# An adaLN block with segmented attention and a gated feed-forward: instruction order by list scheduling at build time, V stationary in column tiles, transposes moved off TensorE

## The chip, the cores and the metric

The kernel runs on one core of one Trainium2 chip. The metric is the device time in microseconds (us). The kernel before takes 308.86 us (median of 3 runs, 307.05 to 309.61). The profile is one further execution, with a span of 305.5 us. In the profile PE is TensorE's matmuls, PEld its weight loads, DVE is VectorE, ACT is ScalarE, POOL is GpSimd and SP is SyncE, which issues most of the DMAs.

## What is computed

The input x is 2048 rows of 448 numbers in bf16. A conditioning vector c gives six modulation vectors. The first half is attention in 16 heads of 28 numbers, in 4 segments of 512 rows. Within a segment it is causal softmax attention. Beside it stands a memory M that sums phi(k) times v over all earlier segments, and each head blends the two. The second half is a feed-forward with 1792 hidden columns.

```
sa, ca, ga, sb, cb, gb = (silu(c) @ w_mod).reshape(6, 448)

h = layernorm(x) * (1 + ca) + sa
q, k, v = h @ wq, h @ wk, h @ wv              # 16 heads of 28, 4 segments of 512 rows
phi(t) = t + 1 where t > 0, else exp(t)
for each segment s:
    p     = softmax(q_s k_s^T / sqrt(28) + causal mask)
    a_dot = p v_s
    a_mem = phi(q_s) M / (phi(q_s) z + 1e-6)  # M and z of the segments before s
    o_s   = g * a_mem + (1 - g) * a_dot       # g = sigmoid(beta), one number for each head
    M, z  = M + phi(k_s)^T v_s, z + sum phi(k_s)
x = x + ga * (o @ wo)

h = layernorm(x) * (1 + cb) + sb
x = x + gb * ((sigmoid(h @ w_gate) * (h @ w_up)) @ w_down)
```

(The reference blends with a_mem = 0 in the first segment, where M and z are zero.)

## The kernel before

The width of 448 is cut into 4 chunks of 112 partitions. Sixteen attention units, 4 segments of 4 head groups, are run through one after the other. Between their steps a queue of other work (`fill`) is served in order, by a quota of estimated TensorE nanoseconds. The parts that the change touches:

```python
# LayerNorm: statistics on VectorE, power -0.5 on GpSimd, normalised rows xn;
# turned on TensorE against an identity, then modulated on the way out of PSUM
def h_chunk(xns, hT, kc, vi, act_kc=(1, 3)):
    pt = m_bf16("lntr")
    for t in range(TPS):
        nc.tensor.transpose(pt[0:KP, t * P:(t + 1) * P], xns[t][:, kc * KP:(kc + 1) * KP], ident[:])      # L229
    if kc in act_kc:
        nc.scalar.activation(hT[:, kc, :], pt[0:KP, 0:L], AF.Identity, scale=..., bias=...)                 # L231
    else:
        nc.vector.tensor_scalar(hT[:, kc, :], pt[0:KP, 0:L], ..., op0=ALU.mult, op1=ALU.add)                # L234

# Q leaves PSUM through ScalarE, K through VectorE
if eng == "act": nc.scalar.copy(dst[:, hc, :], pq[:, 0:L])
else:            nc.vector.tensor_copy(dst[:, hc, :], pq[:, 0:L])                                           # L276

# memory: K turned on TensorE, then phi
ptk = m_bf16("ptk")
for hc in range(NHC):
    nc.tensor.transpose(ptk[:, hc * P:(hc + 1) * P], kT_of[s][:, hc, t * P:(t + 1) * P], ident[:])          # L294
nc.scalar.activation(ek[:], ptk[:, 0:512], AF.Exp)
nc.vector.tensor_scalar(ek[:], ek[:], 1.0, None, op0=ALU.min)                                               # L299
nc.vector.scalar_tensor_tensor(pk_of[s][:, t, :], ptk[:, 0:512], 0.0, ek[:], op0=ALU.max, op1=ALU.add)      # L300

# logits: four heads at once in row tiles; then exp, then the causal mask on GpSimd
nc.tensor.matmul(lg[:, hs, wid:wid + nq], lhsT=kT[r, hc, ...], rhs=qT[r, hc, kb * P:L], tile_position=(HP * hs, 0))
nc.scalar.activation(pT[:, :, w0:w0 + wid], lg[:, :, 0:wid], AF.Exp, scale=scale)                           # L341
nc.gpsimd.affine_select(out=blk, in_=blk, compare_op=ALU.is_ge, fill=0.0, ...)                              # L353

# P times V: P is stationary, V moves, 29 columns in each of 40 matmuls
for qb in range(TPS):
    for hs in range(4):
        for kb in range(qb + 1):
            nc.tensor.matmul(accv[:, qb, hs, 0:ME], lhsT=pT[:, hs, c0:c0 + P],
                             rhs=vt[:, kb, hc * 4 + hs, 0:ME], start=(kb == 0), stop=(kb == qb))            # L366
for qb in range(TPS):                                                                                       # memory read
    nc.tensor.matmul(memv[:, qb, :, 0:ME], lhsT=pq[:, qb * P:(qb + 1) * P], rhs=rm_of[s][:, hc, :, :], ...) # L373
# ... reciprocals, scales, two products (L379 to L399), their sum on GpSimd (L400)

# the output rows turned on TensorE, copied by VectorE
nc.tensor.transpose(op[0:KP, t * P:(t + 1) * P], ou[:, t, :, :]..., ident[:])                               # L408
nc.vector.tensor_copy(oT_of[s][:, hc, :], op[0:KP, 0:L])                                                    # L409

# output projection L415, residual L418; gate L431, tanh L433, up L436, product L439; down L444, residual L448
# wo and wd are scaled by ga and gb/2 on GpSimd: 4 and 14 operations (L496, L504)
```

PSUM is split in a fixed way: one block of 4 banks for the logits, and 4 single banks for all the rest.

Of the kernel before, what the change touches and what calls it, by code (L numbers as in the profile page):

```python
# [13 lines left out]
P = 128  # L14


@with_exitstack
def kernel(
# [24 lines left out]
    KP, NK = 112, 4  # L43
    assert KP * NK == D and H * Dh == D and L == 512 and TPS == 4 and F == NFC * P
    HP = 32
    NHC = 4
    ME = Dh + 1
# [4 lines left out]
    NWARM, TAIL_GU = 24, 9  # L52
    KB_GROUPS = ((0,), (1, 3), (2,))

# [5 lines left out]
    wts = ctx.enter_context(tc.tile_pool(name="wts", bufs=1))  # L60
    pipe = ctx.enter_context(tc.tile_pool(name="pipe", bufs=2))
    work = ctx.enter_context(tc.tile_pool(name="work", bufs=2))
    ps_lg = ctx.enter_context(tc.tile_pool(name="ps_lg", bufs=1, space=bass.MemoryType.PSUM))
    ps_m = ctx.enter_context(tc.tile_pool(name="ps_m", bufs=4, space=bass.MemoryType.PSUM))

    def m_f32(name):
        return ps_m.tile([P, 512], F32, tag="m", name=name)

    def m_bf16(name):
        return ps_m.tile([P, 1024], BF16, tag="m", name=name)  # L70

    deferred = []

    def later(n, fn):
        deferred.append([n, fn])

    def tick():
        for d in deferred:
            d[0] -= 1
        due = [d for d in deferred if d[0] <= 0]  # L80
        deferred[:] = [d for d in deferred if d[0] > 0]
        for d in due:
            d[1]()

    def flush():
        while deferred:
            deferred.pop(0)[1]()


    c_col = const.tile([KP, NK], BF16)  # L90
    nc.sync.dma_start(c_col[:], c.rearrange("o (k p) -> p (o k)", p=KP))
    x_sb = const.tile([P, NSEG * TPS, D], BF16)

    def load_x(eng, t0, t1):
        eng.dma_start(x_sb[:, t0:t1, :], x_dram[t0 * P:t1 * P, :].rearrange("(t p) d -> p t d", p=P))

    load_x(nc.sync, 0, 2)
    load_x(nc.scalar, 2, 4)
    wmod_k = w_mod.rearrange("(k p) n -> p k n", p=KP)

    def load_wm(eng, j):
        t = wts.tile([KP, NK, D], BF16, name=f"wm{j}", tag=f"wm{j % 2}")
        eng.dma_start(t[:], wmod_k[:, :, j * D:(j + 1) * D])
        return t

    wm = {0: load_wm(nc.sync, 0), 1: load_wm(nc.scalar, 1)}
    wq_sb = wts.tile([KP, NK, H, HP], BF16)
    wk_sb = wts.tile([KP, NK, H, HP], BF16)
    wv_sb = wts.tile([KP, NK, D], BF16)
    wo_sb = wts.tile([KP, NK, D], BF16)  # L110
    wg_sb = wts.tile([KP, NK, F], BF16)
    wu_sb = wts.tile([KP, NK, F], BF16)
    wd_sb = wts.tile([P, NFC, D], BF16)
    beta_t = const.tile([P, H], BF16)
    wq_st = wd_sb[0:KP, 0:NK, :].rearrange("p k (h d) -> p k h d", d=Dh)
    wk_st = wd_sb[0:KP, NK:2 * NK, :].rearrange("p k (h d) -> p k h d", d=Dh)
    nc.vector.memset(wq_sb[:, :, :, Dh:HP], 0.0)
    nc.vector.memset(wk_sb[:, :, :, Dh:HP], 0.0)
    nc.sync.dma_start(wq_st, A_wq.rearrange("(k p) (h d) -> p k h d", p=KP, d=Dh))
    nc.scalar.dma_start(wk_st, A_wk.rearrange("(k p) (h d) -> p k h d", p=KP, d=Dh))  # L120
    nc.sync.dma_start(wv_sb[:], A_wv.rearrange("(k p) n -> p k n", p=KP))

    def late_loads():
        load_x(nc.sync, TPS, 2 * TPS)
        nc.sync.dma_start(beta_t[:], A_beta.partition_broadcast(P))
        wm[2] = load_wm(nc.sync, 2)
        load_x(nc.sync, 2 * TPS, 3 * TPS)
        nc.sync.dma_start(wo_sb[:], A_wo.rearrange("(k p) n -> p k n", p=KP))
        wm[3] = load_wm(nc.sync, 3)
        load_x(nc.sync, 3 * TPS, 4 * TPS)  # L130
        for w_sb, w_dram in ((wg_sb, B_w_gate), (wu_sb, B_w_up)):
            wv_ = w_dram.rearrange("(k p) n -> p k n", p=KP)
            nc.sync.dma_start(w_sb[:, 0:2, :], wv_[:, 0:2, :])
            nc.sync.dma_start(w_sb[:, 2:4, :], wv_[:, 2:4, :])
        wm[4] = load_wm(nc.sync, 4)
        nc.sync.dma_start(wd_sb[:], B_w_down.rearrange("(fc p) n -> p fc n", p=P))
        wm[5] = load_wm(nc.sync, 5)


    ident = const.tile([P, P], BF16)  # L140
    nc.gpsimd.memset(ident[:], 0.0)
    nc.gpsimd.affine_select(out=ident[:], in_=ident[:], compare_op=ALU.not_equal, fill=1.0,
                            base=0, pattern=[[-1, P]], channel_multiplier=1)
    mhalf = const.tile([P, TPS], F32)
    nc.gpsimd.memset(mhalf[:], -0.5)
    bmask = const.tile([P, NHC, 4, ME], BF16)
    M_sb = const.tile([P, NHC, 4, ME], F32)
    cols = const.tile([KP, 4, NK], F32)
    coef = const.tile([P, 2, H], F32)

    qT_of = [const.tile([P, NHC, L], BF16, name=f"qT{s}") for s in range(3)]
    qT_of.append(qT_of[0])
    nc.vector.memset(qT_of[2][:, 0, :], 0.0)


    th = const.tile([KP, NK], F32)
    nc.scalar.activation(th[:], c_col[:], AF.Tanh, scale=0.5)
    nc.vector.tensor_scalar(th[:], th[:], 0.5, 0.5, op0=ALU.mult, op1=ALU.add)
    silu = const.tile([KP, NK], BF16)
    nc.vector.tensor_tensor(silu[:], th[:], c_col[:], ALU.mult)  # L160
    vt_all = [const.tile([P, TPS, H, HP], BF16, name=f"vt{s}") for s in range(NSEG)]
    silu_bc = const.tile([KP, NK, P], BF16)

    def late_consts():
        nc.vector.tensor_copy(silu_bc[:], silu[:].rearrange("p (k o) -> p k o", o=1).to_broadcast([KP, NK, P]))
        for s in range(NSEG):
            nc.gpsimd.memset(vt_all[s][:, :, :, Dh:Dh + 1], 1.0)
        nc.scalar.activation(coef[:, 1, :], beta_t[:], AF.Tanh, scale=0.5)
        nc.vector.tensor_scalar(coef[:, 1, :], coef[:, 1, :], 0.5, 0.5, op0=ALU.mult, op1=ALU.add)
        nc.vector.tensor_scalar(coef[:, 0, :], coef[:, 1, :], -1.0, 1.0, op0=ALU.mult, op1=ALU.add)  # L170

        nc.gpsimd.memset(bmask[:], 1.0)
        for hs in range(4):
            nc.gpsimd.affine_select(out=bmask[:, :, hs, :], in_=bmask[:, :, hs, :], compare_op=ALU.is_ge,
                                    fill=0.0, base=-HP * hs, pattern=[[0, NHC], [0, ME]], channel_multiplier=1)
            nc.gpsimd.affine_select(out=bmask[:, :, hs, :], in_=bmask[:, :, hs, :], compare_op=ALU.is_ge,
                                    fill=0.0, base=HP * hs + Dh - 1, pattern=[[0, NHC], [0, ME]],
                                    channel_multiplier=-1)

    def mod_cols(jobs):  # L180
        cp = m_f32("cp")
        for j, vi in jobs:
            for kc in range(NK):
                for k in range(NK):
                    nc.tensor.matmul(cp[0:KP, vi * NK + kc:vi * NK + kc + 1], lhsT=wm[j][:, k, kc * KP:(kc + 1) * KP],
                                     rhs=silu[:, k:k + 1], start=(k == 0), stop=(k == NK - 1))
        for j, vi in jobs:
            src = cp[0:KP, vi * NK:(vi + 1) * NK]
            if vi % 2:
                nc.vector.tensor_scalar(cols[:, vi, :], src, 1.0, None, op0=ALU.add)  # L190
            else:
                nc.vector.tensor_copy(cols[:, vi, :], src)

    def mod_rep(j, mul, name):
        rp = m_f32("rp")
        for k in range(NK):
            nc.tensor.matmul(rp[:, 0:D], lhsT=silu_bc[:, k, :], rhs=wm[j][:, k, :],
                             start=(k == 0), stop=(k == NK - 1))
        rep = const.tile([P, D], BF16, name=name, tag="rep")
        nc.scalar.mul(rep[:], rp[:, 0:D], mul)  # L200
        return rep


    class LN:
        def __init__(self, srcs, key):
            self.srcs, n = srcs, len(srcs)
            self.mv = work.tile([P, n, nc.vector.BN_AGGR_DIM], F32, tag=f"mv{n}", bufs=4, name="mv")
            self.rs = work.tile([P, n], F32, tag=f"rs{n}", bufs=4, name="rs")
            self.out = xns_of.setdefault(key, [])

        def stats(self, i):
            st = work.tile([P, nc.vector.BN_STATS_DIM], F32, tag="st", bufs=4, name="st")
            nc.vector.bn_stats(st[:], self.srcs[i])  # L213
            nc.vector.bn_aggr(self.mv[:, i, :], st[:])
# [283 lines left out]
    def prep_b2():  # L498
        mod_cols(((3, 2), (4, 3)))
# [108 lines left out]
```

The softmax here doesn't subtract the row's maximum and nothing guards it: scores larger than these inputs give would overflow.

## Time and profile before

| | |
|---|---|
| time, median of 3 | 308.86 us |
| span of the profile | 305.5 us |
| ACT, exp of the logits (L341) | 48 operations, mean 1.594 us, busy 76.5 us |
| DVE, product of tanh and up (L439) | 56 operations, mean 0.686 us, busy 38.4 us |
| POOL, causal mask (L353) | 64 operations, mean 0.640 us, busy 40.0 us |
| ACT, tanh (L433) | 56 operations, mean 0.596 us, busy 32.9 us |
| HBM read | 10.67 MB, nearly all of it in the first 60 us |

An engine's busy time is the union of its instructions. A matmul's listed duration (0.389 us for a gate matmul) [...] consecutive ones overlap. For TensorE the distance from the start of one group to the start of the next says more; it is called a slot below. In the slices of the page each digit is one fortieth of the span (7.6 us), and PEclk is the clock that TensorE was granted, in tenths of full speed.

### The profile page before, as it was taken

The page shows a single profiled execution, that of the slowest core. Times are in us where ns is not written, and L with a number is a line of the kernel's source. Part 1 is how long each engine was busy: PE and PEld are TensorE (multiplying, and loading weights), DVE is VectorE, ACT ScalarE, POOL GpSimd, SP SyncE. Part 2 cuts the span into 40 slices and gives each one's busy share as a digit, 9 for nine tenths or more (in the row PEclk, how much of TensorE's full clock was granted, in tenths as well). Part 3 has the DMA queues.
Part 4 walks back from the last instruction along what each step waited for, and adds up shares of the span by engine and source line. Part 5 has one row for each costly group of instructions (what it writes and reads, how often), then busy time and mean ns, then how long its engine had stood idle before and what let it go on. Part 6 is the DMA issues. An engine that isn't in the chain of part 4 may idle for free.

```text
span 305.5 us, 5534 instructions
## 1 busy us (share of the span) xinstructions
PE 277.3 (91%) x2256; PEld 142.9 (47%) x2256; DVE 175.4 (57%) x393; ACT 151.5 (50%) x185; POOL 99.6 (33%) x159
## 2 busy tenths in 40 slices
PE   8888599699886979999998999998999998999995
PEld 3534346284543335545455354444644544544452
DVE  3647694863589535466786254779637558333331
ACT  1456658545955365657436467661675320133300
POOL 0336152713697813131543314326233104000000
PEclk9899999958999689999999799999999999999999
DMA  6999101720000000000001000000100000100001
GB/s 163 280 292 294 58 0 32 233 56 0 3 0 2 0 0 3 0 2 0 2 15 47 0 2 0 4 2 12 35 15 2 0 2 9 37 15 2 0 15 45
DMA packets 12472, 12.84 MB, mean 42 GB/s; under 512 B 1184, under 2 KB 11552, under 8 KB 12448
## 3 DMA queue, kind: packets, MB, share of 16 engines
q1 hardware_dynamic: 11248, 11.48, 13.6%
q10 hardware_dynamic: 1200, 1.03, 1.2%
q8 instruction: 17, 0.28, 0.4%
q14 instruction: 7, 0.06, 0.1%
HBM read 10.67 MB, written 1.84 MB: 41 GB/s over the span
## 4 chain that ended last, share of the span: by engine, by line
PE 66%; DVE 16%; ACT 9%; DMA 3%; issue 3%; POOL 2%; SPq 0%; DVEq 0%; ACTq 0%
PE gps L431 16%; PE ups L436 16%; PE dps L444 13%; PE pq L271 7%; ACT pT L341 5%; PE lg L338 4%; PE acc L366 3%; DMA wd_sb<-in_A_wq_dram 3%; DVE st L213 3%; PE pv L282 2%; DVE x_sb L418 2%; DVE pk L300 2%; DVE pqt L349 2%; ACT hT L231 1%; PE otr L408 1%
## 5 line engine op out<-in xcount | busy, mean ns | idle before, releaser
L341 ACT ACTIVATE pT<-lg 128x2048 bf16<-128x2048 f32 (+1 forms) x48 | 76.5, 1594 | 59.9 <-PE lg L338 59.7
L439 DVE SCALAR_TENSOR_TENSOR fT<-tt,ups 128x512 bf16<-128x512 f32 x56 | 38.4, 686 | 58.2 <-PE ups L436 44.6
L353 POOL TENSOR_SCALAR_AFFINE_SELECT pT<-pT 128x512 bf16<-128x512 bf16 x64 | 40.0, 640 | 68.4 <-ACT pT L341 68.2
L431 PE MATMUL gps<-hT,wg_sb 112*128 112x512 bf16 x224 | 60.1, 389 | 2.0 <-DVE hT L234 0.8
L436 PE MATMUL ups<-hT,wu_sb 112*128 112x512 bf16 x224 | 59.2, 388 | 0.0
L433 ACT ACTIVATE tt<-gps 128x512 f32<-128x512 f32 x56 | 32.9, 596 | 40.4 <-PE gps L431 37.6
L444 PE MATMUL dps<-wd_sb,fT 128*128 128x448 bf16 x224 | 44.2, 353 | 2.3 <-DVE t L393 1.3
L436 PEld LDWEIGHTS <-wu_sb 112*128 112x128 bf16 x224 | 22.0, 100 | 28.7 <-issue 3.3
L431 PEld LDWEIGHTS <-wg_sb 112*128 112x128 bf16 x224 | 20.5, 99 | 27.6 <-issue 5.9
L444 PEld LDWEIGHTS <-fT 128*128 128x128 bf16 x224 | 21.3, 98 | 23.4 <-DVE t L393 1.7
L400 POOL TENSOR_TENSOR ou<-t,t 128x448 bf16<-128x448 f32 x12 | 13.8, 1146 | 53.4 <-DVE t L399 53.4
L271 PE MATMUL pq<-hT,wq_sb 112*128 112x512 bf16 x64 | 19.4, 425 | 5.2 <-DVE pk L300 1.9
L448 DVE TENSOR_TENSOR ot<-dps,x_sb 128x448 bf16<-128x448 f32 x16 | 9.9, 621 | 20.0 <-PE dps L444 20.0
L366 PEld LDWEIGHTS <-pT 128*128 128x128 bf16 x640 | 18.4, 96 | 4.7 <-issue 2.2
L213 DVE BATCH_NORM_STATS2 st<-x_sb 128x6 f32<-128x448 bf16 x32 | 19.8, 618 | 1.1 <-DMA x_sb<-in_A_x_dram 0.6
L271 PE MATMUL pq<-hT,wk_sb 112*128 112x512 bf16 x64 | 19.2, 429 | 0.9 <-DVE x_sb L418 0.9
L366 PE MATMUL acc<-vt,pT 128*128 128x29 bf16 x640 | 18.5, 176 | 1.4 <-DVE pk L300 1.4
L338 PE MATMUL lg<-qT,kT 28*128 28x512 bf16 (+3 forms) x256 | 17.8, 311 | 1.5 <-DVE kT L276 0.8
L231 ACT ACTIVATE hT<-lntr,cols 112x512 bf16<-112x512 bf16 x16 | 11.9, 779 | 14.3 <-PE lntr L229 14.3
L276 DVE CAST kT<-pq 128x512 bf16<-128x512 f32 x16 | 10.9, 679 | 9.8 <-PE pq L271 9.8
L229 PE MATMUL lntr<-ident,xn 128*112 128x128 bf16 x128 | 11.7, 230 | 4.6 <-ACT vt L284 1.8
L274 ACT CAST qT<-pq 128x512 bf16<-128x512 f32 x16 | 9.5, 591 | 12.2 <-PE pq L271 12.1
(78 smaller groups left out, 305.5 us busy)
## 6 DMA issues: line engine op xcount, KB each, us to landing
wm<-in_w_mod_dram SPq DMA_DIRECT2D x5, 392.0 KB, 5.2
out_dram<-ot SPq DMA_DIRECT2D x16, 112.0 KB, 1.7
wg_sb<-in_B_w_gate_dram SPq DMA_DIRECT2D x2, 784.0 KB, 12.4
wu_sb<-in_B_w_up_dram SPq DMA_DIRECT2D x2, 784.0 KB, 15.5
wd_sb<-in_B_w_down_dram SPq DMA_DIRECT2D x1, 1568.0 KB, 8.1
x_sb<-in_A_x_dram SPq DMA_DIRECT2D x3, 448.0 KB, 8.8
wm<-in_w_mod_dram ACTq DMA_DIRECT2D x1, 392.0 KB, 6.1
wd_sb<-in_A_wk_dram ACTq DMA_DIRECT2D x1, 392.0 KB, 8.6
```

The lines of the kernel that those rows point to most:

```text
L213: nc.vector.bn_stats(st[:], self.srcs[i])
L231: nc.scalar.activation(hT[:, kc, :], pt[0:KP, 0:L], AF.Identity, scale=cols[:, vi + 1, kc:kc + 1], bias=cols[:, vi, kc:kc + 1])
L271: nc.tensor.matmul(pq[:, 0:L], lhsT=head_cols(w_sb, k, hc), rhs=h[:, k, :], start=(k == 0), stop=(k == NK - 1))
L338: nc.tensor.matmul(lg[:, hs, wid:wid + nq], lhsT=kT[r, hc, kb * P:(kb + 1) * P], rhs=qT[r, hc, kb * P:L], start=True, stop=True, tile_posi ...
L341: nc.scalar.activation(pT[:, :, w0:w0 + wid], lg[:, :, 0:wid], AF.Exp, scale=scale)
L353: nc.gpsimd.affine_select(out=blk, in_=blk, compare_op=ALU.is_ge, fill=0.0, base=0, pattern=[[0, 4], [1, P]], channel_multiplier=-1)
L366: nc.tensor.matmul(accv[:, qb, hs, 0:ME], lhsT=pT[:, hs, c0:c0 + P], rhs=vt[:, kb, hc * 4 + hs, 0:ME], start=(kb == 0), stop=(kb == qb))
L431: nc.tensor.matmul(gp[:, 0:L], lhsT=wg_sb[:, k, fs], rhs=h[:, k, :], start=(k == 0), stop=(k == NK - 1))
L433: nc.scalar.activation(tt[:], gp[:, 0:L], AF.Tanh, scale=0.5)
L436: nc.tensor.matmul(up[:, 0:L], lhsT=wu_sb[:, k, fs], rhs=h[:, k, :], start=(k == 0), stop=(k == NK - 1))
L439: nc.vector.scalar_tensor_tensor(ft[:], tt[:], 1.0, up[:, 0:L], op0=ALU.add, op1=ALU.mult)
L444: nc.tensor.matmul(dp[:, 0:D], lhsT=fT_of[(s, fc)][:, t * P:(t + 1) * P], rhs=wd_sb[:, fc, :], start=(fc == 0), stop=(fc == NFC - 1))
```

## The change

The kernel is written anew around the same mathematics.

- **Order.** Every piece of work becomes a node with an engine, an estimated duration, predecessors, and slots that it takes from rings of buffers. A list scheduler runs over them at build time and fixes the order of instructions on each engine. All eight PSUM banks are one pool; the logits take four neighbouring ones. Attention units are released at a fixed pace (`T0`, `STEP`, in nanoseconds), and further constants set priorities.
- **Transposes.** LayerNorm rows and phi(k) are turned by DMA (the first segment's LayerNorm 1 stays on TensorE). Attention sums and outputs are turned by VectorE in blocks of 32 by 32.
- **P times V.** V is the stationary side, 32 columns wide, in four column tiles, one for each head; P moves. The memory read turns its sides as well.
- **Modulation of LayerNorm 1** goes into the weights: wq, wk and wv are scaled by 1 + ca when they are loaded, and the shift becomes a bias row. LayerNorm 2 is modulated in SBUF after the transposes.
- **Chunks** of the width are 128, 128, 128 and 64, padded with zeros to 128, instead of four of 112.
- **Smaller moves.** K leaves PSUM through ScalarE. phi is taken as min(exp(t), max(t, 0) + 1), from SBUF. The down sums are three nodes each.

The diff, cut to its core:

```diff
+PRM = dict(T0=13000.0, STEP=9100.0, lg=71000, ex=-12000, mask=97000, wo=30000, tanh=22500, up=-2000, f=57500,
+           dn=-27800, phi=27000, t=1000, ln1=-18000, mem=-33000, pj=-4000, ot=-83000)
+class Graph:
+    LAG = {"PE": {"PE": 0, "ACT": 260, "DVE": 320, "POOL": 320, "SP": 320}, ...}
+    def run(self):
+        self.ranks()
+        ...
+                ready = sorted((n for n in avail[e] if self.ready_at(n) <= t), key=lambda n: -(n.rank + n.prio))
+        ...
+        for n in order:
+            if n.fn is not None:
+                n.fn()
...
-    ps_lg = ctx.enter_context(tc.tile_pool(name="ps_lg", bufs=1, space=bass.MemoryType.PSUM))
-    ps_m = ctx.enter_context(tc.tile_pool(name="ps_m", bufs=4, space=bass.MemoryType.PSUM))
+    ps = psum.tile([P, 8, 512], F32, name="ps")
+    G.pool("bank", 8)
...
+    def bias_row(st, dst, loads, prio, pad):      # sa @ w, 4 matmuls of 448 for each of wq, wk, wv
+    def scaled(st, dst, loads, eng, prio, pad):   # w * (1 + ca), 4 operations for each, on ACT, DVE, POOL
...
+        b = pool_op(860 if w == 1 else 1330, rstd, stats, prio, use=[mv])
+            n = dve(290, ...)                     # normalise
+    def transposed(xn, n, hT, t, first, prio=0):
+            nc.sync.dma_start_transpose(hT_r[:, hT.at, :, t * P:(t + 1) * P], xn_r[:, xn.at, :])
+        return add("SP", 500, fn, [n, first], ..., lag=2200, prio=prio)
...
+    def phi(src, dst, deps, slots, take, prio):
+        a = act(520, lambda: nc.scalar.activation(e_r[:, e.at, 0, :], src(), AF.Exp), ...)
+        b = dve(340, lambda: nc.vector.tensor_scalar(e_r[:, e.at, 1, :], src(), 0.0, 1.0, op0=ALU.max, op1=ALU.add), ...)
+        return dve(340, lambda: nc.vector.tensor_tensor(dst(), e_r[:, e.at, 0, :], e_r[:, e.at, 1, :], ALU.min), ...)
+    def memory(s):
+            tr = add("SP", 500, lambda f2=f2, pk=pk: nc.sync.dma_start_transpose(
+                pk_r[:, pk.at, :, :], pq_r[:, f2.at, :]), [n], take=[pk], use=[f2], lag=2200)
...
-                    nc.tensor.matmul(accv[:, qb, hs, 0:ME], lhsT=pT[:, hs, c0:c0 + P],
-                                     rhs=vt[:, kb, hc * 4 + hs, 0:ME], start=(kb == 0), stop=(kb == qb))
+            e = act(1800 if wid == L else 960, ex, [n], use=[lg, pT], prio=PRM["ex"])
+        def pv():
+            for kb in range(TPS):
+                for hs in range(4):
+                    nc.tensor.matmul(pf(acc)[hs * HP:(hs + 1) * HP, kb * P:L], lhsT=vt_r[:, v.at, kb, hc * 4 + hs, :],
+                                     rhs=pT_r[:, pT.at, hs, OFF[kb]:OFF[kb] + L - kb * P],
+                                     start=(kb == 0), stop=(kb == TPS - 1), tile_position=(0, HP * hs),
+                                     skip_group_check=True)
+        def back(b, i):
+            nc.vector.transpose(A_r[:, A.at, i, :, :].rearrange("p b e -> p (b e)"), pf(b))
+            m = add("PE", 220, lambda: nc.tensor.matmul(pf(mem), lhsT=rm_r[:, rm.at, :], rhs=pq_r[:, pq.at, :], ...
+            m1 = dve(1030, lambda: nc.vector.tensor_tensor(U_r[:, U.at], A_r[:, A.at, :, :, 0:Dh], bc(0, 2), ALU.mult), ...
+            m = pool_op(1150, lambda: nc.gpsimd.tensor_tensor(O_r[...], U_r[:, U.at, 0], U_r[:, U.at, 1], ALU.add), ...
+        return dve(400, lambda: nc.vector.transpose(oT_r[:, oT.at, hc, :], O_r[:, O.at]...), ...
...
+            v_n[(s, t)] = act(430, ...)           # V out of PSUM
+            def mod(kc=kc):                       # LayerNorm 2, in SBUF, after all four transposes
+                nc.vector.tensor_scalar(v, v, cols[..., 3, kc:kc + 1], cols[..., 2, kc:kc + 1], op0=ALU.mult, op1=ALU.add)
+        PARTS = ((0, 5), (5, 10), (10, 14))       # a down sum in three nodes
+            on.append(attention(s, hc, oT, lambda g, i=s * NHC + hc: PRM["T0"] + PRM["STEP"] * (i + g / 3.0), ...))
+    G.run()
```

## The prediction

> **What bounds the kernel now.** I read the page's busy times first, and then its slices: which engine is fullest, and when.
>
> ```profile
> PE 277.3 (91%) x2256; PEld 142.9 (47%) x2256; DVE 175.4 (57%) x393; ACT 151.5 (50%) x185; POOL 99.6 (33%) x159
> ...
> PE   8888599699886979999998999998999998999995
> ...
> DVE  3647694863589535466786254779637558333331
> ACT  1456658545955365657436467661675320133300
> ...
> PEclk9899999958999689999999799999999999999999
> ```
>
> TensorE is fullest, but overlapping matmuls are in those 91%. So I took slots from its timeline, from one group's start to the next one's, in a stretch without waits (start, duration, then the group):
>
> ```profile
> 179.08 1.03 PE L436 MATMUL ups<-hT,wu_sb 112*128 112x512 bf16 x4
> 179.94 1.16 PE L366 MATMUL acc<-vt,pT 128*128 128x29 bf16 x40
> 180.94 0.37 PE L373 MATMUL mem<-rm,pqt 128*128 128x116 bf16 x4
> 181.25 0.40 PE L338 MATMUL lg<-qT,kT 28*128 28x384 bf16 x8
> 181.58 1.04 PE L431 MATMUL gps<-hT,wg_sb 112*128 112x512 bf16 x4
> 182.45 1.03 PE L436 MATMUL ups<-hT,wu_sb 112*128 112x512 bf16 x4
> ```
>
> P times V, 40 small matmuls, has a slot of 1.00 us, the memory read 0.31, eight row-tiled logits matmuls 0.33, a 512-wide matmul 0.216. Elsewhere in this view a 448-wide one has 0.189 (56 in 10.61), a transpose about 0.067 (16 of L229 in 1.26 less a tail of some 0.2), one of L294 0.055, a memory-update matmul 0.061, a modulation matmul 0.057. At full clock, in us: gate and up 448 x 0.216 = 96.9; down 224 x 0.189 = 42.4; Q and K 128 x 0.216 = 27.7; V and output projection 128 x 0.189 = 24.2; logits 16 x (0.33+0.33+0.22) = 14.1; P times V 16.0; memory read 3.7; LayerNorm transposes 8.6; output transposes 4.3; key transposes 2.6; memory update 2.9; modulation 5.1; warm-up 5.2. That is **253.7 us of the span of 305.5**. The windows of 5 us (PE, weight loads, DVE, ACT, POOL, then granted clock) show where the other 52 go:
>
> ```profile
> 55.00:60.00 5.00, 2.25 (x15) 1.12 (x14) 4.69 (x11) 2.87 (x5) 3.14 (x4) 1.00 0.85 262
> 60.00:65.00 5.00, 4.80 (x37) 3.23 (x36) 4.13 (x10) 2.02 (x2) 1.99 (x3) 0.54 0.01 2
> 95.00:100.00 5.00, 2.79 (x19) 1.20 (x19) 4.79 (x13) 2.46 (x2) 3.32 (x7) 0.80 0.01 3
> 100.00:105.00 5.00, 5.00 (x16) 1.55 (x15) 3.89 (x11) 0.99 (x2) 4.15 (x7) 0.52 0.00 0
> 175.00:180.00 5.00, 5.00 (x32) 2.38 (x31) 1.45 (x3) 4.11 (x6) 1.27 (x2) 1.00 0.00 0
> ```
>
> Where VectorE is full (4.69 and 4.79 of 5), TensorE starves, and in the next window its clock falls to about half. Five microseconds times the missing clock, over all windows, is 13.7 us. Before the first matmul and around the modulation lie 2.5 us, after the last one 3.4. The remaining **32 us are waits in order**, nearly all between 15 and 125 us; from 175 on TensorE hardly waits.
>
> [...] Here eight row-tiled matmuls stream 2048 columns in 0.33 us where single ones would need 0.865: 2.6x. [...] the same VectorE operation beside GpSimd work and later in a free stretch:
>
> ```profile
> 53.45 4.05 POOL L496 TENSOR_TENSOR wo_sb<-wo_sb,ga 112x448 bf16<-112x448 bf16 x4
> ...
> 54.48 1.14 DVE L299 TENSOR_SCALAR ek<-ek 128x512 bf16<-128x512 bf16 x1 [1.35 <-ACT ek L296]
> ...
> 60.42 0.28 DVE L299 TENSOR_SCALAR ek<-ek 128x512 bf16<-128x512 bf16 x1
> ```
>
> **The change part by part, TensorE.** (a) LayerNorm transposes: all but 16 of 128 go to DMA, -112 x 0.067 = -7.5. (b) Output transposes go to VectorE, -4.3. (c) Key transposes go to DMA, -2.6. (d) P times V: V is stationary in four column tiles, and 40 matmuls become 16 that stream (512+384+256+128) = 1280 columns on each tile. At 0.216/512 us per column, 5120 columns are 2.16 us on one tile; [...] 16 x (1.00-0.70) = -4.8. (e) The memory read becomes one 512-wide matmul: 12 x (0.31-0.24) = -0.8. (f) The modulation's shift becomes a bias row: 12 more 448-wide matmuls at the start, +2.3. Sum: -17.7, so **236.0 us at full clock**. Projections, gate, up and down, 191 us of it, stay.
>
> **The other engines.** VectorE loses the K copies (10.9), three LayerNorms' modulation from PSUM (8.0), the old accumulation arithmetic (30.3 over the rows of lines 379 to 399, plus 2.5), the output copies (6.7) and the old phi (25.9). It gains, per attention unit after the first segment: two turns of 128x512 float32 out of PSUM at about 0.66 (the row of the K copy, same shape, has 0.68), reciprocal and scale 0.47, one product of 896 elements 1.05, a turn of the output 0.45, phi 0.70: 4.0, times 12 = 48. The first segment's units cost 2.15 each, 8.6; phi of the keys 12 x 0.7 = 8.4; memory 12 x 0.43 = 5.2; LN2 modulation from SBUF 16 x 0.33 = 5.3; start work some 8. With what stays (both LayerNorms' statistics and normalisation 38.5, products 38.4, two residual additions 19.7) that is **about 180 us, 175 before**. ScalarE: +9.5 for the K copies, -10.5 for modulation, +3 for weights: about 157, 151 before. GpSimd: about 106. So no engine is relieved; the gain must come from TensorE's 17.7 and from the waits.
>
> **The order.** A list scheduler with measured-looking durations replaces quotas. Its releases set the pace: the last logits go out at 13 + 9.1 x 15.67 = 156 us; before they ended at about 234. By then, of the sums above, VectorE must have done all but two segments' products and two down sums: about 147 of 160 us. ScalarE must have done all but 28 tanh of 0.60: 141 of 160. TensorE must have done all but two segments' feed-forward (2 x 38 us): 160 of 160. Three engines nine tenths full or more and each strictly in order cannot run without slips. Some of the scheduler's figures are below the rows: exp 1.80 against 1.88, norm 0.29 against 0.42, V copy 0.43 against 0.54. I take 5 to 8% of 160 us, **13 us of waits** instead of 32. The half-clock stretches follow long waits; with fewer waits, and without the 32 one-column matmuls at 63 us, I take **5 us instead of 13.7**. Start and end stay at 6: Q still needs weights, modulation and the scaling of the weights first.
>
> Sum: 236 + 6 + 13 + 5 = **260 us**, 49 less than the 308.86 measured (the span is 3 us shorter than that time; I leave this inside the range).
>
> **Rivals.** First, *the DMA transposes become the wait.* 40 of them, 128 KB each, planned at 0.5 us to issue and 2.2 to land. The page of before has 1.7 us for a plain 112 KB store, but loads issued in a crowd took 7 to 15. If a transpose took 5 us, each LN2 (4 segments) and each later LN1 (3) would wait some 3 us more, and TensorE could drop to half clock after it: 15 to 25 us, 275 to 285 in all. Against it: only the last LN2 lacks other work to hide it, and the loads (10.67 MB) end before most transposes. Second, *VectorE becomes the bound of the first 160 us.* For it: 147 of 160[...] beside GpSimd's 18 scaling operations of 1.05 and 12 additions of 1.15, its fast operations can triple. It would stretch the phase by 10 to 20 us: 270 to 280. Third, *the removed TensorE work was only part of waits anyway and the waits stay:* then only the 17.7 and the clock come off at most, 285 to 290. Against it: the waits sit behind single stalled operations in order (K copies, phi, residual adds), just what a better order mends. Fourth, *all goes as planned:* 236 plus 10: 246.
>
> **Range and chances.** The first two rivals together make the upper side longer: 246 to 282. To be no faster, the change would have to add over 40 us of new waits to work that got smaller; only serialisation by the transposes, or by dependences between slots of the one large PSUM tile, could do that. Faster 0.93, same 0.03, slower 0.04.
>
> **What would show each step.** Right: TensorE's row at 9 from about 15 us on, and the clock row hardly under 9; slots of P times V near 0.7; no transposes on TensorE after 15 us; the last exp before 170 us, then 75 to 80 us of gate, up and down alone; DVE near 180 us busy. Wrong: waits of TensorE on DVE or DMA behind LN2; transposes landing later than 3 us; P times V at 1 us or more, if column tiles do not run at once; gaps at regular 9 us, which would make the release pace and not an engine the bound; a clock under 0.9 in spite of full slices.

## The result and the profile after

The kernel after takes **280.37 us** (median of 4 runs, 280.26 to 281.19), the kernel before 307.96 us in the same session (4 runs). The ratio is 0.912, with a 95% interval of 0.908 to 0.916. That is faster, and inside the range of the prediction, but the gain is 27.6 us where 49 were forecast.

The page of the kernel after, the lines that answer to those of before:

```profile
PE 250.2 (90%) x1600; PEld 111.1 (40%) x1624; DVE 192.1 (69%) x395; ACT 150.7 (54%) x191; POOL 113.5 (41%) x200
...
PE   5994977969998999989989997999999999999992
...
DVE  5684469799998999999699997346885422441433
...
PEclk9998887997999999999999999999999999999998
```

From slice 26 on (174 us) TensorE stands at 9. In slices 9 to 24 (56 to 167 us) VectorE's digits are now 9 but for two, where they were mostly 3 to 8. VectorE has 192 us of work, 12 more than forecast. The windows of the attention stage (columns: sum, PE, weight loads, DVE, ACT, POOL, granted clock, DMA share, GB/s) say it in microseconds. First the kernel after, then the same windows of the kernel before:

```profile
50.00:110.00 60.00, 55.29 (x410) 23.26 (x406) 56.36 (x105) 49.44 (x64) 39.10 (x51) 0.97 0.20 36
110.00:170.00 60.00, 53.90 (x399) 23.00 (x404) 55.45 (x115) 41.56 (x44) 28.60 (x46) 1.00 0.15 27
...
50.00:110.00 60.00, 50.58 (x464) 28.52 (x457) 38.75 (x84) 35.76 (x44) 36.16 (x47) 0.86 0.15 42
110.00:170.00 60.00, 55.57 (x518) 28.64 (x518) 36.81 (x87) 34.28 (x38) 20.28 (x32) 0.97 0.03 9
```

VectorE went from 38.8 and 36.8 of 60 us to 56.4 and 55.5.

TensorE's own work came out as forecast. Its timeline (start, duration, then the group) gives the new slots:

```profile
100.58 0.73 PE L704 MATMUL ps<-pT,vt 128*32 128x512 bf16 x16
101.24 0.39 PE L718 MATMUL ps<-pq,rm 128*128 128x512 bf16 x1
101.47 1.03 PE L782 MATMUL ps<-hT,wg_sb 128*128 128x512 bf16 x3
```

From 100.58 to 101.24 is 0.66 us for P times V (forecast 0.70, before 1.00), and the memory read has 0.23 (forecast 0.24). With these two the sum of the prediction becomes 235 us of TensorE at full clock. (The trace lists 1600 of 1624 matmuls; the sum counts all.) The span of 277.6 us then splits as follows; "rest" is what remains, waits above all.

| us | before | predicted | after |
|---|---|---|---|
| TensorE at full clock | 253.7 | 236 | 235 |
| clock not granted, (1 - mean clock) x span | 13.7 | 5 | 8.1 |
| ahead of the first and behind the last matmul | 5.9 | 6 | 8.5 |
| rest | 32 | 13 | 26 |

(The 5.9 of before hold 1 us of waiting around the modulation.) So TensorE's share of the gain is there in full, part of the clock's is there, and the rest has shrunk by 6 us instead of 19.

The list of waits says for whom TensorE stood still in the kernel after (us in all, times, longest). The first two lines lie before 50 us, the last two between 50 and 178 us, where the last exponential begins:

```profile
PE ps L681 <- ACT pT L691: 2.9, 2, 1.5
PE ps L704 <- POOL pT L696: 1.9, 1, 1.9
...
PE ps L622 <- DVE A L711: 3.6, 3, 2.3
PE ps L782 <- DVE fT L792: 3.1, 4, 1.9
```

With the smaller lines of these lists, 7.5 us lie between the first matmul and 50 us, 5.3 of them for ScalarE, and 9.8 between 50 and 178 us, 9.6 of them for VectorE. Behind 178 us there is none. About 9 of the 26 us stand in no wait and stay unexplained. The experiments ask about the middle stretch.

### The profile page after: what moved, and what is told of

Its sections match the earlier page's. It is cut to its first block, busy times and chain, and to the rows that moved or that the text cites. A ratio compares the mean times of both kernels' runs of the same rounds, so it can differ in the third digit from the quotient of the medians.

```text
span 277.6 us, 4458 instructions
## 1 busy us (share of the span) xinstructions
PE 250.2 (90%) x1600; PEld 111.1 (40%) x1624; DVE 192.1 (69%) x395; ACT 150.7 (54%) x191; POOL 113.5 (41%) x200
## 5 line engine op out<-in xcount | busy, mean ns | idle before, releaser
L691 ACT ACTIVATE pT<-ps 128x2048 bf16<-128x2048 f32 (+1 forms) x48 | 76.2, 1599 | 18.6 <-PE ps L681 16.5
L787 ACT ACTIVATE tt<-ps 128x512 f32<-128x512 f32 x56 | 33.2, 597 | 76.7 <-PE ps L782 75.2
L792 DVE SCALAR_TENSOR_TENSOR fT<-tt,ps 128x512 bf16<-128x512 f32 x56 | 37.7, 681 | 32.4 <-PE ps L782 29.9
L782 PE MATMUL ps<-hT,wg_sb 128*128 128x512 bf16 x217 | 57.0, 379 | 3.5 <-DVE fT L792 3.1
L782 PE MATMUL ps<-hT,wu_sb 128*128 128x512 bf16 x213 | 56.4, 379 | 1.6 <-DVE A L711 0.9
L805 PE MATMUL ps<-wd_sb,fT 128*128 128x448 bf16 x224 | 45.4, 353 | 0.7 <-DVE A L711 0.6
L782 PEld LDWEIGHTS <-wg_sb 128*128 128x128 bf16 x224 | 21.3, 98 | 29.1 <-issue 5.3
L782 PEld LDWEIGHTS <-wu_sb 128*128 128x128 bf16 x224 | 21.6, 98 | 27.2 <-issue 2.9
L742 POOL TENSOR_TENSOR O<-U 128x448 bf16<-128x448 f32 x12 | 13.7, 1141 | 36.2 <-DVE U L740 36.2
L681 PE MATMUL ps<-qT,kT 28*128 28x512 bf16 (+3 forms) x256 | 18.2, 313 | 3.2 <-ACT pT L691 2.9
L711 DVE STREAM_TRANSPOSE A<-ps 128x512 f32<-128x512 f32 x28 | 18.7, 693 | 2.1 <-PE ps L704 2.1
L601 PE MATMUL ps<-hT,wq_sb 128*128 128x512 bf16 x61 | 17.6, 411 | 1.1 <-ACT pT L691 0.7
```

What stands on the lines that cost most here:

```text
L601: nc.tensor.matmul(pf(b), lhsT=w_sb[:, kc, hc * 4:(hc + 1) * 4, :].rearrange("p h e -> p (h e)"), rhs=hT_r[:, hT.at, kc, :], start=(kc == ...
L681: nc.tensor.matmul(ps[:, lg.at + hs, o:o + nq], lhsT=kT_r[r, k.at, hc, kb * P:(kb + 1) * P], rhs=qT_r[r, q.at, hc, kb * P:L], start=True, ...
L691: nc.scalar.activation(pT_r[:, pT.at, :, w0:w0 + wid], ps[:, lg.at:lg.at + 4, 0:wid], AF.Exp, scale=scale)
L711: nc.vector.transpose(A_r[:, A.at, i, :, :].rearrange("p b e -> p (b e)"), pf(b))
L782: nc.tensor.matmul(pf(b), lhsT=w_sb[:, k, fs], rhs=hT_r[:, hT.at, k, :], start=(k == 0), stop=(k == NK - 1))
L787: a = act(560, lambda gp=gp, tt=tt: nc.scalar.activation(tt_r[:, tt.at, :], pf(gp), AF.Tanh, scale=0.5), [n1], use=[gp, tt], prio=PRM["tanh"])
```

## The experiments

Theory A: VectorE sets the pace of 50 to 170 us, and GpSimd stretches VectorE's operations. Theory B: TensorE's work, or the release pace of the schedule, sets it. Later ones are named where they come up. In most runs every other instruction keeps its place. In four the constants of the schedule are searched anew and the order changes with them: the old back end, LayerNorm 2 turned on TensorE, the other order and the measured durations.

All runs at a glance. Ratio is to the kernel before in the same session, with its 95% interval; the last three columns are from one profile each, with the rest worked out as above (start and end 8.5 us). The kernel before took 307.4 to 308.7 us (medians) in the four sessions, so a difference of about 1 us between two runs says nothing.

| run | us | ratio | TensorE sum | clock | rest |
|---|---|---|---|---|---|
| after | 280.4 | 0.912 (0.908 to 0.916) | 235 | 8.1 | 26 |
| no masks | 272.2 | 0.882 (0.876 to 0.888) | 235 | 5.4 | 21 |
| down weights not scaled | 274.2 | 0.888 (0.882 to 0.895) | 235 | 7.6 | 21 |
| turns twice | 298.6 | 0.969 (0.961 to 0.976) | 235 | 9.8 | 43 |
| P times V twice | 281.8 | 0.913 (0.905 to 0.921) | 245.6 | 4.5 | 21 |
| old back end | 276.3 | 0.898 (0.893 to 0.903) | 244 | 6.3 | 15 |
| LayerNorm 2 turned on TensorE | 279.8 | 0.911 (0.904 to 0.919) | 239 | 5.0 | 26 |
| other order | 281.8 | 0.916 (0.910 to 0.922) | 235 | 8.6 | 27 |
| modulation on ScalarE | 279.2 | 0.906 (0.900 to 0.912) | 235 | 1.9 | 30 |
| load early | 279.1 | 0.905 (0.899 to 0.911) | 235 | 6.4 | 26 |
| gate at the end | 278.6 | 0.903 (0.897 to 0.910) | 235 | 9.4 | 24 |
| load early, gate at the end | 276.8 | 0.901 (0.892 to 0.910) | 235 | 6.6 | 24 |
| measured durations | 280.8 | 0.911 (0.903 to 0.919) | 235 | 14.0 | 22 |

### More work for VectorE, more work for TensorE

```diff
-            nc.vector.transpose(A_r[:, A.at, i, :, :]..., pf(b))
+            for _ in range(2):
+                nc.vector.transpose(A_r[:, A.at, i, :, :]..., pf(b))
```

> Each of the 28 VectorE turns of an attention sum is done twice: 28 x 0.69 = 19.4 us more VectorE work, all of it in the attention stage, same data. Theory A: VectorE has no slack there, and the time grows by 15 to 20 us, to 295 to 300. Rival B (TensorE or the release pace binds): the slack of the stage takes most of it, below 8 us more, 281 to 288.

```diff
-            for kb in range(TPS):
+            for kb in (*range(TPS), *range(TPS)):
                 for hs in range(4):
                     nc.tensor.matmul(pf(acc)[...], lhsT=vt_r[...], rhs=pT_r[...], ...)
```

> P times V is done twice in each of the 16 units: 16 x 0.66 = 10.6 us more TensorE slots (four column tiles), same result. Theory A: TensorE idles 10 to 15 us between 50 and 170 us while VectorE is full, so the time grows by 2 to 5 us only, to 282 to 285. Rival B (TensorE is the bound throughout): the full 10.6 us, 290 to 292.

19.4 us more of VectorE cost 18.2 us; 10.6 us more of TensorE cost 1.4 us. TensorE's waits for VectorE, from 50 us to the last exponential, rise from 9.6 to 23.6 us with the doubled turns. With the doubled product they are 7.0; there a part of the 10.6 us was also met by the clock, of which 4.5 us were not granted instead of 8.1. In the attention stage TensorE has idle time to give away and VectorE, busy for 56.4 and 55.5 us of each 60, has next to none. Theory B falls.

### Less work for GpSimd

Both leave out work that GpSimd does beside VectorE, so neither computes the whole of the reference: the first leaves out the causal masks, the second the gate of the feed-forward branch.

```diff
-                masks.append(pool_op(650, mask, [e], ...))
+                masks.append(pool_op(650, None, [e], ...))
```

> Leaves out the causal masks (64 GpSimd operations, 42.4 us of GpSimd); the order of everything else stays. Theory A: the attention stage (50 to 170 us) is bound by VectorE, whose SBUF operations are stretched by GpSimd [...] (about 20 us over their fastest durations). Then DVE busy falls by 8 to 14 us, the last exp comes earlier and the time falls by 6 to 12 us, to 268 to 274. Rival B (TensorE bound by its own slots, or the release pace binds): DVE may shrink, but the time changes by less than 3 us, 277 to 281. Rival C (the wait of P times V for the last mask binds): the time falls, but DVE busy stays within 3 us of 192.

```diff
-    W_d = [pool_op(1050, lambda k=k: nc.gpsimd.tensor_tensor(wd_sb[:, k, :], wd_sb[:, k, :], rep[:, 1, :], ALU.mult),
+    W_d = [pool_op(1050, None,
```

> Leaves out the 14 GpSimd products that scale w_down by gb/2 (14.8 us of GpSimd, between about 50 and 90 us); the order stays. Theory A: the VectorE operations that lie beside them (up to 1.1 us each instead of 0.3 to 0.4) shrink by 4 to 7 us in all, and the time falls by 3 to 6 us, to 274 to 277. Rival B: below 2 us of change, since VectorE is not what binds there; 278 to 281.

Without the masks 8.2 us come off, without the 14 products 6.2, though GpSimd is busy for only 41% of the span and nothing waits for those products until much later. VectorE's busy time falls by 7.1 us without the products, as theory A had it. Without the masks it falls by 5.9, less than the 8 to 14 of theory A: the products are still there, and the normalisations keep their mean of 0.56 us. Rival C, the wait for the last mask, has a small part in the 8.2 us: in the kernel after P times V waits for a mask once, 1.9 us at 39 us, and exponentials 1.3 us in all. How much of the 8.2 us is the stretching of VectorE and how much these waits is not separated; the products, which nothing waits for, are the cleaner case.

The timeline shows how their 6.2 us come about. First the kernel after:

```profile
55.01 1.19 POOL L519 TENSOR_TENSOR wd_sb<-wd_sb,rep 128x448 bf16<-128x448 bf16 x1
...
55.24 3.76 DVE L546 TENSOR_SCALAR xn<-x_sb,mv,rs 128x448 bf16<-128x448 bf16 x4
...
56.80 3.09 POOL L519 TENSOR_TENSOR wd_sb<-wd_sb,rep 128x448 bf16<-128x448 bf16 x3
...
63.05 1.21 PE L622 MATMUL ps<-wv_sb,hT 128*128 128x448 bf16 x4 [2.33 <-DVE A L711]
```

Then the same normalisations and the same matmuls without the products:

```profile
53.79 2.08 DVE L546 TENSOR_SCALAR xn<-x_sb,mv,rs 128x448 bf16<-128x448 bf16 x4
...
60.43 0.92 PE L622 MATMUL ps<-wv_sb,hT 128*128 128x448 bf16 x4
```

With the products TensorE stands still for 2.33 us until a VectorE turn is done, and its clock from 60 to 70 us is 0.83; without them this wait is gone and the clock there is 1.00. Four normalisations take 3.76 us beside the products and 2.08 us beside masks alone; where GpSimd is idle one takes 0.38 us (mean of six). Over all 32 normalisations of the kernel after the mean is 0.56 us, and 1.10 for the two that ran beside products alone, about the 1.08 of a product. Other operations keep their time there: the product of tanh and up takes 0.68 us with a mask beside it or without, the turn of an attention sum 0.69 alone and 0.70 beside a product, the output's turn 0.69 alone and 0.70 beside a mask. Why some stretch and others do not was not shown.

### How late the chip runs against the schedule

The kernel computes a start time for every piece of work when it is built. The start of an exponential in the trace minus its start in that schedule says where time is lost. If VectorE's sum of work alone counted, lateness would grow evenly through the stage; it does not. (Schedule time in the head line, us late below it; the last column is the span minus the schedule's end.)

| schedule at | 18.7 | 47.3 | 57.3 | 83.9 | 106.8 | 157.7 | end |
|---|---|---|---|---|---|---|---|
| after | 2.6 | 7.6 | 12.2 | 13.6 | 13.5 | 20.2 | 24.3 |
| no masks | 2.6 | 6.7 | 9.6 | 9.4 | 8.6 | 12.4 | 16.5 |
| down weights not scaled | 1.8 | 7.8 | 8.3 | 8.3 | 7.8 | 14.3 | 18.4 |
| turns twice | 1.5 | 7.8 | 16.0 | 20.2 | 21.9 | 36.5 | 42.8 |
| modulation on ScalarE | 2.5 | 4.9 | 10.5 | 13.3 | 13.2 | 18.0 | 22.3 |
| load early, gate at the end | 2.3 | 7.4 | 7.9 | 7.9 | 7.4 | 14.2 | 20.8 |

The kernel after loses 5 us between 19 and 47 us of its schedule, 4.6 in the ten microseconds in which GpSimd scales the down weights, almost nothing from 57 to 107, and 6.7 from there to the last exponential. Without the products the second loss is gone: 0.5 us in each of the three runs without them, 3.9 to 5.6 in the four that have them in the same order and otherwise change little there (the kernel after, P times V twice, load early, modulation on ScalarE). Without the masks the third loss is 3.8. Ahead of the first product single profiles differ for no such reason: at 41.2 us of the schedule the kernel after, the run without products, the modulation on ScalarE and the gate at the end have all done the same work, and are 5.0 to 7.9 us late.

### Undoing P times V and the turns

P stationary as in the kernel before, no VectorE turns, the outputs turned on TensorE; the rest of the change stays.

```diff
-                    nc.tensor.matmul(pf(acc)[hs * HP:(hs + 1) * HP, kb * P:L], lhsT=vt_r[...], rhs=pT_r[...], tile_position=(0, HP * hs), ...)
-            nc.vector.transpose(A_r[:, A.at, i, :, :]..., pf(b))
-        return dve(400, lambda: nc.vector.transpose(oT_r[:, oT.at, hc, :], ...), ...)
+                        nc.tensor.matmul(rows(acc)[:, qb, hs, 0:Dh + 1], lhsT=pT_r[..., c0:c0 + P], rhs=vt_r[...], ...)
+                nc.tensor.transpose(pb(ob)[:, t * P:(t + 1) * P], O_r[...], ident[:])
+        return dve(380, lambda: nc.vector.tensor_copy(oT_r[:, oT.at, hc, :], pb(ob)[:, 0:L]), ...)
```

> The back end of attention is put back to that of the kernel before: probabilities stationary (40 matmuls a head group), no VectorE turns, TensorE transposes of the outputs; the constants of the ordering are searched anew for this program, whose own schedule then ends at 259.7 us (253.3 in the kernel after). TensorE gains about 9 us of slots (16 x 0.35 for the products, 16 x 0.24 for the transposes), VectorE loses about 20 us (30 us of turns and 27 us of products and reciprocals out, some 34 us of smaller ones and copies in). Theory A (VectorE, stretched by GpSimd, sets the pace of 50 to 170 us): faster than the kernel after, 268 to 276 us, VectorE's row no longer near 9. Rival B (TensorE's work and the schedule's own end set it): 6 to 9 us slower than after, 286 to 290 us.

Its page:

```profile
PE 257.4 (94%) x2108; PEld 127.4 (46%) x2108; DVE 176.1 (64%) x400; ACT 150.5 (55%) x191; POOL 113.2 (41%) x200
...
PE   5984999998989999999998999999999999999992
```

It takes 276.3 us, 4.1 less than the kernel after, though TensorE has 9 us more to do, and its interval (up to 0.903) lies below that of the kernel after (from 0.908). VectorE has lost 16 us, TensorE's row is at 9, a few times 8, from slice 5 on, and the rest of the split falls from 26 to 15 us. TensorE's waits for VectorE fall from 9.6 to 2.5 us. So this part of the change, each kernel with an order made for it, costs time. The gain is just short of what theory A expected (268 to 276 us); TensorE's work is 9 us longer, which takes back a part.

```diff
-    trs.append(transposed(xn, ln, hT, t, ...))            # by DMA, then modulation in SBUF on VectorE
+    nc.tensor.transpose(pb(tb)[:, t * P:(t + 1) * P], ...) # then modulation out of PSUM, half ScalarE, half VectorE
```

> The second LayerNorm's 16 DMA transposes are replaced by TensorE transposes into PSUM, with the modulation done on the way out (half on ScalarE, half on VectorE); ordering constants searched anew, own schedule 257.1 us. TensorE +4 us, VectorE about -4 us, ScalarE +5. Theory A: within 4 us of the kernel after (276 to 284 us), as the DMA transposes cost hidden time. Rival 1 of the prediction (the DMA transposes behind the second LayerNorm are a wait on the path): 8 us or more faster, below 273 us. If TensorE's own time were the bound: 284 us.

279.8 us, the same as after and far from rival 1's 273: the DMA transposes behind LayerNorm 2 were not the wait.

### The order and its durations

```diff
-PRM = dict(T0=13000.0, STEP=9100.0, lg=71000, ex=-12000, mask=97000, ...)
+PRM = dict(...)          # other constants, schedule 253.2 us instead of 253.3
```

> The kernel after with other constants of the ordering (found by a search from another start), same instructions, own schedule 253.2 us as before; it shows how far the order alone moves the time. Theory A: the same bound in another order, 276 to 285 us. If the order of the kernel after is itself the cause of the lost time, a second order of equal planned length will be off by more than 6 us, most likely slower (286 us and more).

281.8 us: another order of the same length loses the same time (25.6 us against its schedule). The order of the kernel after is not an unlucky one.

```diff
-            n = dve(290, lambda t=t, src=src, xn=xn: nc.vector.tensor_scalar(   # normalise
+            n = dve(420, lambda t=t, src=src, xn=xn: nc.vector.tensor_scalar(
-        return dve(400, lambda: nc.vector.transpose(oT_r[:, oT.at, hc, :], ...), ...)
+        return dve(690, lambda: nc.vector.transpose(oT_r[:, oT.at, hc, :], ...), ...)
```

> The kernel after, same instructions; the scheduler that orders them at build time is given the durations measured in its trace (normalization 420 instead of 290 ns, turns 690 instead of 620 and 400, the parts of the feature map 400 to 635 instead of 340 to 520, and so on; VectorE 195 us in all instead of 174) and its constants are searched anew: own schedule 254.4 us. Theory D (the schedule lost its 20 us on the chip because it was made with VectorE durations that are too short): 265 to 273 us. Theory A (contention comes and goes with what lies beside it, and no mean duration foresees it; the bound stays): 275 to 282 us.

280.8 us, so theory D's 265 to 273 is missed, but in an instructive way. The schedule made with 195 us of VectorE work is only 1.1 us longer (254.4), and between 108 and 156 us of it the chip loses 0.8 us, where the kernel after lost 6.7 in the like stretch. The time goes elsewhere: 8 us before 47 us of the schedule, and 7.1 between 73 and 79 us of it, where its GpSimd products now lie. Theory A's range holds (275 to 282). Its windows there, columns as above:

```profile
85.00:90.00 5.00, 2.77 (x12) 0.68 (x16) 5.00 (x6) 1.97 (x3) 5.00 (x6) 0.71 0.14 28
90.00:95.00 5.00, 3.73 (x16) 1.39 (x10) 4.57 (x9) 2.31 (x3) 2.64 (x4) 0.50 0.00 0
```

And its timeline in the same place:

```profile
84.08 3.24 POOL L518 TENSOR_TENSOR wd_sb<-wd_sb,rep 128x448 bf16<-128x448 bf16 x3 [0.39 <-ACT rep L423]
...
85.31 3.83 DVE L766 TENSOR_SCALAR hT<-hT,cols 128x512 bf16<-128x512 bf16 x4
...
86.49 0.39 PE L781 MATMUL ps<-hT,wg_sb 128*128 128x512 bf16 x1 [0.42 <-DVE hT L766]
```

The products stretch the four modulations behind LayerNorm 2 to 3.83 us (where GpSimd is idle one takes 0.40 us in the kernel after), TensorE waits for each of them in turn and is busy 2.77 of 5 us, and then its clock is granted at 0.50. One collision is paid twice, as in the kernel before (2.25 of 5 us busy, then a clock of 0.54).

### Smaller moves

```diff
-                nc.vector.tensor_scalar(v, v, cols[..., 3, kc:kc + 1], cols[..., 2, kc:kc + 1], op0=ALU.mult, op1=ALU.add)
+                nc.scalar.activation(v, v, AF.Identity, scale=cols[..., 3, kc:kc + 1], bias=cols[..., 2, kc:kc + 1])
```

> The modulation of the second LayerNorm (16 VectorE operations, 7.8 us) runs on ScalarE instead, in the same places of the order: VectorE -8 us (6 of them before 170 us), ScalarE +10 us. Theory A: 4 to 7 us faster than the kernel after, 273 to 277 us. Rival: ScalarE is as tight as VectorE, or the wait for the transposes now holds up the exponentials: no gain, 280 to 285 us.

279.2 us, with an interval that overlaps that of the kernel after: neither side's number. One VectorE operation of 0.49 us became one of 0.81 on ScalarE:

```profile
L767 ACT ACTIVATE hT<-hT,cols 128x512 bf16<-128x512 bf16 (+1 forms) x16 | 12.2, 813 | 0.0
```

VectorE lost 5.6 us, ScalarE gained 9.7, and of the 2.7 us that this run was ahead at 47 us of its schedule (its clock from 20 to 50 us is 0.94, that of the kernel after 0.83) all but 0.3 was gone at 107. From 50 us to the last exponential TensorE's waits for VectorE fell from 9.6 to 7.6 us, but those for ScalarE rose from 0.2 to 3.0. So a microsecond taken off VectorE is not always one off the time: here the wait passed on to ScalarE.

```diff
+                order.remove(n)                                   # n: the load of segment 3's rows
+                order.insert(min(i for i, o in enumerate(order) if o.turn), n)   # ahead of the first DMA transpose
```

> Order kept; only the load of the fourth segment's rows is issued ahead of the first DMA transpose on the SyncE queue (in the kernel after it stands behind transposes that wait for their inputs, and VectorE then waits 4.9 us for it at 36.6 us). Measured against its own schedule the kernel after falls 5 us behind between 34 and 50 us. Theory C1 (that wait is on the path): 3 to 5 us faster than after, 275.5 to 277.5 us. Rival: VectorE has room there and the delay comes from the TensorE clock (0.68 in 40 to 50 us), or is caught up in the full stage behind it: within 1.5 us of after, 279 to 282 us.

In the kernel after, the list of waits had VectorE waiting for this load:

```profile
DVE st L533 <- DMA x_sb<-in_A_x_dram: 9.5, 4, 4.9
```

(us in all, times, longest). In the new run that wait is 2.1 us in all, longest 1.2. Yet the time is 279.1 us and its interval overlaps that of the kernel after; at 47 us of the schedule it is 7.1 us late instead of 7.6. Most of the early loss is therefore not that load. TensorE's clock between 20 and 50 us is 0.83 in the kernel after (0.68 from 40 to 50) and 0.83 here. In the profile of the run with the modulation on ScalarE it was 0.94, and the loss between 19 and 47 us of the schedule was 2.4 us instead of 5; which of the two causes the other was not tried.

```diff
-    W_d = [pool_op(1050, lambda k=k: nc.gpsimd.tensor_tensor(wd_sb[:, k, :], wd_sb[:, k, :], rep[:, 1, :], ALU.mult),
+    W_d = [pool_op(1050, None,
...
-            a = dve(600, lambda ...: nc.vector.tensor_tensor(ot_r[:, ot.at, :], pf(b)[:, 0:D], x_sb[:, i, :], ALU.add), ...)
+                nc.vector.tensor_tensor(ot_r[:, ot.at, :], pf(b)[:, 0:D], rep[:, 1, :], ALU.mult)
+                nc.vector.tensor_tensor(ot_r[:, ot.at, :], ot_r[:, ot.at, :], x_sb[:, i, :], ALU.add)
```

> Order kept; the gate of the second branch is no longer multiplied into the 14 blocks of the down weights on GpSimd (50 to 83 us), but into the 16 outputs on VectorE (one bf16 product and one sum more each, 0.4 to 0.6 us; 3 of the 16 stand before 170 us, the rest where VectorE has room). The full computation. Theory A (GpSimd's weight products stretch VectorE where it is full): leaving them out was worth 6.2 us; here 1.5 us come back before 170 us and 0.5 at the end: 274.5 to 277.5 us. Rival (VectorE's sum of work alone counts): VectorE's work hardly changes (about -7 +8), 279 to 282 us.

278.6 us, 1.8 less than after where at least 3 were expected; the intervals overlap. Until 107 us of the schedule it is as little late as without the products (8.5 us), so theory A's mechanism is there. Then it loses 8.8 us up to the last exponential, where the run without the products lost 6.5; three of the added operations stand there, and in this profile the clock between 140 and 170 us was 0.94. Behind it, it loses another 6.6 us against 4.1. The added operation (0.41 us) makes the row of last outputs longer, and I had put only 0.5 us for it.

The last run has both edits, the early load and the gate at the end.

> The two together, full computation, order kept. If the gains add: 4 + 4 us, 271 to 274.5 us. If the later stage swallows the early load's gain: 275 to 278 us.

276.8 us, 3.6 less than after: below either single move and inside the range for a gain that the later stage swallows (275 to 278), short of the full sum (271 to 274.5). Its interval overlaps that of the kernel after. It is 6.0 us less late at the last exponential and gives 2.5 back behind it. With the old back end (276.3 us) it is the fastest version here that computes all of the reference. The two together were not tried.

## Why the prediction was right in its direction and wrong in its size

- **TensorE, -17.7 us: right.** Forecast 236.0, found 235; 0.66 for P times V against 0.70, and 0.23 for the memory read against 0.24. The 0.70 was the author's estimate, which no run of before showed; at the 2.6 times of the row-tiled logits it would have been 0.83. One tile would need an estimated 2.16 us for the 5120 columns, at the 0.216 us that 512 take in the kernel before, so at 0.66 four column tiles do run at once.
- **Clock, 5 us instead of 13.7: half right.** It is 8.1, of which 5 lie before 50 us, where the mean clock is 0.90. The row still falls under 9 in slices 4 to 7 and 10 (21 to 49 and 62 to 69 us).
- **Start and end, 6 us: 8.5.** 3.3 ahead of the first matmul, 5.2 behind the last.
- **VectorE, "about 180 us, 175 before": the step that failed.** It is 192.1. The 180 is a sum of groups, the 175 a busy time in which neighbours that overlap count once. As sums of groups it was 186.7 before and is 204.3 after, so the forecast saw less work for VectorE where there was 17.6 us more. The attention units with their phi were put at 65 us and hold 80 (groups added up); LayerNorm 38.5 and 42.7; memory 5.2 and 9.6. The mis-sized terms are the ones below. They are normalisation and phi, which stretch beside GpSimd (a normalisation takes 0.38 us alone and 1.10 beside a product, phi's last step 0.42 and 1.08), and the output's turn.

```profile
L711 DVE STREAM_TRANSPOSE A<-ps 128x512 f32<-128x512 f32 x28 | 18.7, 693 | 2.1 <-PE ps L704 2.1
L546 DVE TENSOR_SCALAR xn<-x_sb,mv,rs 128x448 bf16<-128x448 bf16 x32 | 17.2, 563 | 3.3 <-POOL rs L541 3.2
L636 DVE TENSOR_TENSOR pq<-e 128x512 bf16<-128x512 bf16 x24 | 13.8, 575 | 5.3 <-DMA pk<-pq 2.6 <-ACT e L633 1.0
...
L744 DVE STREAM_TRANSPOSE oT<-O 128x512 bf16<-128x512 bf16 x16 | 11.0, 697 | 1.1 <-POOL O L742 1.1
```

(After the bar stand busy us and mean ns, then idle time before.) The turn out of PSUM was put at 0.66 us and takes 0.69. The output's turn was put at 0.45 and takes 0.70. phi's two VectorE parts were put at 0.70 together and take 0.99. The 0.45 and the 0.70 were the author's estimates; no run of before held these operations in this form.

- **VectorE "147 of 160" and ScalarE "about 157": sums that do not come out.** 180 less the two segments' 28 products of 0.686 and 8 down sums of 0.621 leaves 156 of 160, so by its own terms VectorE had no room. ScalarE's terms (151.5 + 9.5 - 10.5 + 3) make 153.5; it is 150.7.
- **Waits, "5 to 8% of 160 us, 13": failed in part for that reason.** They are 26. TensorE's waits for VectorE, 9.6 us, are the part that the runs explain. The 7.5 us before 50 us, mostly for ScalarE, and the 9 that stand in no wait are not explained by them. That GpSimd stretches VectorE was in the prediction, under the second rival, but as a rival and not as a term of the sum. The runs show what it is worth: 6.2 us for the weight products; the 8.2 for the masks hold direct waits too.
- **Rival 1, the DMA transposes: not borne out.** They land 2.5 us after issue, near the plan of 0.5 to issue and 2.2 to land (the page's list of DMA issues; median at the end of the line), and turning LayerNorm 2 on TensorE changes nothing (279.8 us against 280.4).

```profile
hT<-xn SPq DMA_TRANSPOSE x28, 2.5
```

- **Rival 2, VectorE as the bound of the first 160 us: this is what came, from 50 us on,** and the time lies just above its 270 to 280 us. Doubling the turns and the old back end show it from both sides. **Rival 3, the waits stay: half true,** 32 became 26. A release pace as the bound is ruled out by the doubled turns: a pace set by the constants would have hidden part of them.
- **Signs.** TensorE's row "at 9 from about 15 us on": wrong before 170 us. "Last exp before 170 us, then 75 to 80 us": the last one began at 177.9, and 99 us of span followed it. (The schedule itself had 96 us between the start of that exponential and its end.)

## What to carry to other kernels

A change that moves work from the fullest engine to a second one must be sized with the second engine's durations beside its neighbours, not alone: here 9 us of TensorE were bought with 16 us of a VectorE that then had no room. A forecast that adds up groups must be compared with groups added up, not with a busy time. When an order is fixed at build time, subtract its planned starts from the starts in the trace: the few places where lateness jumps say more than the sums of busy time. Work that nothing waits for, on an engine that is 41% busy, still cost 6.2 us here; ask what stands beside it on the other engines just then, and how long that takes alone: 0.38 us for a normalisation, where it took 1.10.

## What the runs showed of the hardware that was not expected

- A VectorE turn in 32x32 blocks of 128x512 takes the same time in bf16 out of SBUF (0.697 us) as in float32 out of PSUM (0.693).
- The cost of GpSimd beside VectorE differed with the kind of both. A normalisation of 128x448 in bf16 takes 0.38 us alone, 0.57 to 0.75 beside masks and 1.10 beside products of two SBUF tensors; a turn out of PSUM takes 0.69 to 0.70 in all three cases (means).
- Sixteen matmuls on four column tiles that stream 5120 columns in all have a slot of 0.66 us. At the 0.216 us that 512 columns take in the kernel before, one tile would need an estimated 2.16: 3.3 times as long.
